# Seven transposes of the last chunks moved from TensorE to transposing transfers on SyncE's queue, in a kernel of an RWKV-7 recurrence and a squared-ReLU feed-forward network

## The chip, the cores and the metric

The kernel runs on one core of a Trainium2 chip. The metric is the device time of the whole program in microseconds, taken over several executions. A profiled execution gives, beside its own time, a span from the first to the last instruction; the rest of that execution's time lies around the span.

## The reference

For 4 batches of 8 heads, 768 steps and a head dimension of 40, a state of 40 x 40 per head is carried from step to step; then all heads' outputs go through a feed-forward network with squared ReLU.

```python
for t in range(S):
    y[:, :, t] = np.einsum('bhd,bhde->bhe', rt, state)
    Sa = np.einsum('bhde,bhe->bhd', state, at)
    state_decay = state * wt[:, :, None, :] - np.einsum('bhd,bhe->bhde', Sa, bt)
    state = state_decay + np.einsum('bhd,bhe->bhde', vt, kt)
...
h = x @ w_in              # x: 3072 tokens x 320, w_in: 320 x 2048
r = np.maximum(h, 0.0)
return (r * r @ w_out).astype(np.float32)
```

Inputs and output are float32; the kernel multiplies in bfloat16.

## The kernel before

The 768 steps are cut into 12 chunks (`c` = 0 to 11) of 64 steps (`L`), all 32 heads side by side. Each chunk goes through five functions that record named operations: `load` (`ldw`, `ldk`, `ldb`, `ldv`, `lda`, `ldr`: DMAs on SyncE's queue), `prep` (decays and turned copies), `rec` (the recurrence inside the chunk and the new state), `read` (the chunk's outputs) and `ffn`. An operation's name holds its kind, the chunk and a part: `TV 11` is the transpose of chunk 11's v and u.

What is to be turned, and who reads it:

- `TK c` (in `prep`): `KB`, k over b, scaled by the decay, is transposed by TensorE into PSUM, and `tK c` copies it to `KBT`. `EN c g0` and `EN c g1` read it.
- `TV c` (in `read`): `VU`, v over u, is transposed, and `tV c` copies it to `VUT`. `CX c g0` and `CX c g1` read it. u comes from `u1 c`, which follows `NU c`.
- `TS c` (in `rec`): the state after the chunk, `STb`, is transposed, and `tS c` copies it to `Sb`. `RS c+1` of the next chunk reads it.

From chunk 4 on each of these transposes is 32 TensorE instructions of 64 rows (line 394); chunks 0 to 3 (`WHOLE`) use 16 of 128 rows (line 397). All other matmuls are recorded at line 390. `F c u0` to `u3` and `FL c u0` to `u3` are the first product of the feed-forward network (8 and 4 matmuls), `f` and `q` the ReLU and the square, `O c u0` to `u3` the second product (8 matmuls each), `o c` its copy into `osb`, `st c` the store (two DMAs on SyncE's queue). For chunk 11 `O` is split in three (`OA`, `OB`, `OC`). `cf c` and `ci c` are products with a triangle of ones that sum the logarithms of the decay, `S`, `SC`, `AS`, `EV`, `NU`, `Y` small products of the recurrence, `XT` the transpose of the outputs for the network.

The weights are loaded at the start through buffers that are in use later (`lwi`, `lwl`, `lwo`) and cast (`cwi`, `cwl`, `cwo`).

There is no scheduler at run time: `ORDER` is a text that names every operation once with its engine (and, for TensorE, one of four PSUM slots), and `Plan.issue` records them in that order. Each engine, SyncE's queue among them, works through its own entries in order and waits for what each one reads. An engine may run ahead of another only as far as data and buffers allow. Two copies of most buffers are used in turn (`c % 2`).

TensorE's instructions have shapes of four kinds (64 or 128 rows by 64 or 128 columns, the `mode` of an operation).

Of the kernel before, what the change touches and what calls it, by code (L numbers as in the profile page):

```python
# [91 lines left out]
DVE mEN 0 g0; SP ldb 2; ACT castA 1; SP lda 2; PE2 EV 0; DVE bK 0; PE0 TA 1; ACT u0 0; SP ldv 1;
DVE tA 1 g1; ACT eg 1; PE NU 0; PE3 TK 1; POOL castR 0; ACT u1 0 g0; DVE tK 1 g0; ACT ln 2; PE1 TR
0; ACT u1 0 g1; POOL hi 2; DVE tA 1 g0; SP lwi 0 k1 x2; ACT tRw 0; POOL lo 2; DVE tK 1 g1; SP ldk
2; PE2 EN 1 g0; PE0 TV 0; ACT castB 2; DVE mEN 1 g0; POOL castA 2; SP ldw 3; PE3 S 0 g0; ACT tV 0;
PE S 0 g1; PE1 EN 1 g1; POOL castV 1 g1; DVE s 0 q0; PE2 BK 1; DVE s 0 q1; ACT castV 1 g0; PE0 ci
2; SP lwi 0 k0 x2; DVE mEN 1 g1; PE3 CX 0 g1; SP lwi 0 k1 x1; ACT exw 2; SP ldr 1; ACT castK 2;
DVE mCX 0 g1; PE0 cf 2; PE1 TK 2; ACT eg 2; SP lwi 0 k0 x3; PE3 AS 1; ACT ef 2; PE EV 1; SP lwi 0
k1 x0; DVE tK 2 g1; SP lwi 0 k0 x0; ACT bK 1; PE0 TS 0; DVE u0 1; SP lwi 0 k1 x3; SP lwi 0 k0 x1;
DVE tK 2 g0; ACT ln 3; PE NU 1; SP ldv 2; ACT tS 0; PE2 CX 0 g0; POOL hi 3; DVE mCX 0 g0; PE1 TA  # L100
2; POOL lo 3; SP lwl 0; ACT u1 1 g0; PE0 SC 1; DVE tA 2 g1; ACT u1 1 g1; PE S 1 g0; PE2 Y 0; DVE
tA 2 g0; POOL castR 1; SP ldk 3; PE S 1 g1; DVE y 0; PE3 TR 1; PE1 EN 2 g1; DVE yd 0; ACT tRw 1;
DVE s 1 q0; POOL cwi 0 k1h0; PE2 EN 2 g0; DVE mEN 2 g1; PE3 TV 1; POOL cwi 0 k0h0; DVE mEN 2 g0;
PE1 BK 2; ACT tV 1; DVE s 1 q1; POOL castV 2 g1; PE2 XT 0; SP lwo 0 x0; POOL castV 2 g0; DVE xt 0;
PE0 ci 3 h0; PE3 ci 3 h1; DVE bK 2; PE2 AS 2; ACT ei 3 h1; PE EV 2; DVE cwi 0 k1h1; POOL cwl 0;
ACT ei 3 h0; PE1 F 0 u0; SP lwo 0 x1; ACT u0 2; ACT ex 3 h0 g0; PE FL 0 u0; SP ldr 2; ACT ex 3 h0
g1; PE NU 2; DVE f 0 u0; ACT ex 3 h1 g0; PE0 CX 1 g1; ACT ex 3 h1 g1; ACT cwi 0 k0h1; SP lda 3;
PE3 FL 0 u1; DVE u1 2 g0; PE F 0 u1; DVE mCX 1 g1; ACT u1 2 g1; PE1 SC 2; SP ldb 3; PE S 2 g0; ACT
f 0 u1; PE2 cf 3; DVE cwo 0 x0; PE0 CX 1 g0; ACT ef 3; PE S 2 g1; DVE mCX 1 g0; POOL cwo 0 x1; PE3
TV 2; PE2 TS 1; DVE s 2 q0; ACT tV 2; SP lwo 0 x2; DVE s 2 q1; PE0 F 0 u2; DVE tS 1; SP lwo 0 x3;  # L110
PE FL 0 u2; ACT castR 2; SP ldv 3; PE1 RS 1; PE Y 1; ACT castA 3; PE2 FL 0 u3; ACT f 0 u2; PE F 0
u3; DVE mulKB 3 h0; POOL mulKB 3 h1; PE3 TA 3; DVE y 1; ACT f 0 u3; PE0 TR 2; DVE yd 1; DVE tA 3
g0; PE1 XT 1; ACT tRw 2; SP ldr 3; PE2 TK 3; DVE xt 1; ACT cwo 0 x2; DVE tA 3 g1; POOL cwo 0 x3;
PE1 FL 1 u1; DVE tK 3; SP ldw 4; PE F 1 u1; POOL q 0 u1; PE3 CX 2 g1; ACT f 1 u1; PE0 CX 2 g0; DVE
mCX 2 g1; PE2 F 1 u2; ACT castV 3 g0; POOL castV 3 g1; SP lwo 0 x4; PE FL 1 u2; DVE mCX 2 g0; PE3
EN 3 g0; ACT f 1 u2; PE1 F 1 u0; POOL castR 3; SP lwo 0 x5; DVE mEN 3 g0; POOL q 0 u0; PE0 EN 3
g1; SP ldk 4; PE FL 1 u0; PE2 RS 2; DVE mEN 3 g1; PE Y 2; PE3 AS 3; ACT ln 4; ACT f 1 u0; PE0 FL 1
u3; DVE hi 4; PE EV 3; DVE yd 2; DVE lo 4; PE F 1 u3; ACT u0 3; POOL cwo 0 x4; DVE y 2; SP lda 4;
PE NU 3; ACT f 1 u3; PE2 ci 4 h0; POOL cwo 0 x5; DVE u1 3 g0; PE1 TS 2; ACT ex 4 h0 g1; SP ldb 4;
POOL q 0 u2; ACT ei 4 h0; DVE u1 3 g1; PE0 O 0 u0; ACT ex 4 h0 g0; ACT tS 2; PE2 ci 4 h1; POOL q 0  # L120
u3; PE3 TV 3; SP lwo 0 x6; ACT ex 4 h1 g0; ACT ei 4 h1; PE1 SC 3; DVE tV 3; ACT ex 4 h1 g1; SP lwo
0 x7; PE S 3 g0; PE S 3 g1; POOL castA 4; SP ldw 5; PE2 TR 3; DVE s 3 q1; PE O 0 u1; ACT tRw 3;
DVE s 3 q0; POOL mulKB 4 h0; PE3 XT 2; PE2 CX 3 g0; ACT xt 2; PE1 cf 4; DVE mCX 3 g0; PE O 0 u2;
ACT ef 4; SP ldv 4; DVE mulKB 4 h1; ACT cwo 0 x6; PE2 TA 4; PE1 CX 3 g1; POOL cwo 0 x7; DVE tA 4
g1; PE3 TK 4; DVE tA 4 g0; POOL q 1 u1; ACT tK 4; PE O 0 u3; DVE mCX 3 g1; PE2 F 2 u0; SP ldw 6;
DVE o 0; ACT q 1 u2; PE3 F 2 u2; DVE q 1 u0; ACT ln 5; PE0 EN 4 g0; PE FL 2 u2; DVE mEN 4 g0; PE1
FL 2 u3; POOL hi 5; ACT f 2 u2; PE FL 2 u0; SP ldr 4; PE F 2 u3; POOL lo 5; ACT f 2 u0; PE3 RS 3;
DVE f 2 u3; SP ldb 5; PE Y 3; POOL castV 4 g0; PE2 FL 2 u1; PE0 cf 5; DVE yd 3; POOL castV 4 g1;
DVE y 3; PE1 EN 4 g1; ACT ef 5; PE F 2 u1; POOL q 2 u0; DVE mEN 4 g1; PE3 XT 3; SP lda 5; ACT f 2
u1; PE0 TS 3; DVE xt 3; ACT ln 6; PE3 ci 5 h1; SP ldk 5; DVE tS 3; PE2 ci 5 h0; ACT ei 5 h1; PE1  # L130
AS 4; POOL hi 6; PE EV 4; ACT ex 5 h1 g1; POOL castR 4; ACT ei 5 h0; PE0 O 1 u0; DVE u0 4; ACT ex
5 h1 g0; POOL q 1 u3; SP lda 6; ACT ex 5 h0 g1; ACT ex 5 h0 g0; PE NU 4; PE O 1 u1; ACT u1 4 g0;
SP ldw 7; POOL lo 6; ACT u1 4 g1; PE2 SC 4; PE S 4 g0; PE S 4 g1; POOL castA 5; DVE mulKB 5 h1;
PE1 TR 4; PE3 ci 6 h1; ACT tR 4 g1; POOL mulKB 5 h0; SP ldr 5; PE O 1 u2; DVE s 4 q0; ACT ei 6 h1;
PE O 1 u3; ACT ex 6 h1 g0; DVE s 4 q1; SP ldv 5; ACT tR 4 g0; POOL q 2 u1; ACT ex 6 h1 g1; PE2 TS
4; ACT o 1; PE3 cf 6; DVE tS 4; PE1 TA 5; ACT ef 6; PE0 TV 4; SP ldr 6; DVE tA 5 g1; POOL castA 6;
PE2 TK 5; DVE tA 5 g0; ACT tV 4; PE3 FL 3 u1; POOL castR 5; PE F 3 u1; DVE tK 5; SP ldb 6; PE1 F 3
u0; DVE f 3 u1; ACT ln 7; PE FL 3 u0; PE0 TR 5; POOL castV 5 g0; ACT f 3 u0; PE2 EN 5 g0; SP lda
7; PE3 FL 3 u3; DVE mEN 5 g0; POOL q 2 u2; PE F 3 u3; ACT tR 5 g1; ACT tR 5 g0; PE1 CX 4 g0; PE2
CX 4 g1; ACT f 3 u3; DVE mCX 4 g0; SP ldk 6; PE0 O 2 u0; POOL q 3 u1; ACT q 2 u3; DVE mCX 4 g1;  # L140
PE3 EN 5 g1; PE1 ci 6 h0; PE O 2 u1; ACT ex 6 h0 g0; SP st 0; DVE mEN 5 g1; ACT castV 5 g1; ACT hi
7; PE2 RS 4; PE Y 4; SP ldv 6; ACT ei 6 h0; POOL lo 7; PE3 AS 5; DVE yd 4; ACT ex 6 h0 g1; PE EV
5; DVE y 4; PE O 2 u2; ACT u0 5; DVE mulKB 6 h1; POOL mulKB 6 h0; ACT q 3 u0; PE2 TA 6; SP ldw 8;
PE NU 5; DVE tA 6 g1; PE O 2 u3; DVE tA 6 g0; ACT u1 5 g0; ACT u1 5 g1; PE2 ci 7 h1; DVE o 2; PE1
XT 4; PE3 TV 5; ACT ex 7 h1 g0; POOL castV 6 g0; ACT ex 7 h1 g1; DVE xt 4; PE0 TK 6; SP ldk 7; ACT
ei 7 h1; DVE tV 5; POOL castA 7; PE1 SC 5; ACT tK 6; PE S 5 g0; POOL q 3 u3; PE S 5 g1; PE2 F 4
u2; DVE s 5 q0; DVE s 5 q1; PE FL 4 u2; ACT castR 6; PE3 CX 5 g0; SP lda 8; PE0 F 3 u2; DVE mCX 5
g0; ACT f 4 u2; PE1 EN 6 g0; SP ldb 7; PE FL 3 u2; DVE mEN 6 g0; PE3 EN 6 g1; ACT f 3 u2; PE2 FL 4
u3; PE F 4 u3; DVE mEN 6 g1; ACT ln 8; PE0 CX 5 g1; PE1 FL 4 u1; ACT f 4 u3; SP st 1; PE F 4 u1;
DVE mCX 5 g1; ACT castV 6 g1; PE2 RS 5; SP ldw 9; PE3 AS 6; ACT f 4 u1; DVE q 3 u2; PE Y 5; PE EV  # L150
6; DVE y 5; POOL mulKB 7 h1; PE1 ci 7 h0; ACT u0 6; DVE yd 5; PE0 cf 7; SP ldr 8; ACT ei 7 h0; PE
NU 6; ACT ex 7 h0 g0; PE2 O 3 u0; DVE u1 6 g0; ACT ex 7 h0 g1; ACT ef 7; SP ldv 7; DVE mulKB 7 h0;
PE O 3 u1; ACT u1 6 g1; DVE q 4 u1; PE0 TA 7; PE3 TR 6; PE1 TK 7; SP ldk 8; ACT tR 6 g0; PE O 3
u2; DVE tK 7; ACT hi 8; ACT tR 6 g1; POOL lo 8; PE O 3 u3; DVE tA 7 g0; DVE tA 7 g1; PE3 XT 5; ACT
o 3; PE1 TV 6; POOL castV 7 g1; DVE xt 5; PE0 ci 8 h0; ACT castR 8; DVE tV 6; PE2 SC 6; PE S 6 g0;
ACT ex 8 h0 g1; PE S 6 g1; ACT ei 8 h0; PE3 F 5 u0; DVE s 6 q0; SP ldr 10; ACT ex 8 h0 g0; DVE s 6
q1; PE FL 5 u0; PE0 CX 6 g1; ACT f 5 u0; PE1 TS 5; DVE mCX 6 g1; SP ldb 8; PE2 FL 5 u1; PE F 5 u1;
# [929 lines left out]
```

## Time and profile before

| what | us |
|---|---|
| median of 3 runs | 245.29 (245.1 to 246.02) |
| the profiled execution | 245.21 |
| its span | 242.8 |
| TensorE busy in it | 223.2 |
| VectorE, ScalarE, GpSimd busy | 182.8, 178.8, 119.9 |

Engines in the profile: PE is TensorE's matmul, PEld its weight loads, DVE is VectorE, ACT ScalarE, POOL GpSimd, SP SyncE; a name with q (SPq, ACTq) is that engine's queue, where it issues or waits. A row of a timeline has the start in us, the time from the first start to the last end, engine, line, operation, written and read tiles, and how many instructions it merges. Since matmuls overlap, the step from one row's start to the next row's start is what a row costs TensorE, and its duration is a little longer.

### The profile page before, as it was taken

The numbers are of one execution on the slowest core, as the hardware profiler recorded it, in microseconds if no ns is written. First come the engines' busy times: TensorE is split into PE (matmuls) and PEld (weight loads), VectorE is DVE, ScalarE is ACT, GpSimd is POOL, SyncE is SP. The second block draws the span as 40 slices with busy tenths as digits, with TensorE's granted clock in tenths as the row PEclk, the third lists the DMA queues.
The fourth block names the chain that finished last, engine by engine and source line by source line (L and its number), as shares of the span: only waits on it lengthen the run. The fifth ranks groups of instructions, "written<-read, shape, count | busy, mean of one in ns | idle before, by whom it ended". The sixth has DMA issues, their size and how long they took to land.

```text
span 242.8 us, 12250 instructions
## 1 busy us (share of the span) xinstructions
PE 223.2 (92%) x5584; PEld 175.7 (72%) x5584; DVE 182.8 (75%) x227; ACT 178.8 (74%) x231; POOL 119.9 (49%) x110
## 2 busy tenths in 40 slices
PE   0587698899999999999999999999999999999994
...
DMA  6989899989978979997864957788457020000403
GB/s 144 232 165 211 191 248 188 227 186 209 196 182 135 196 160 185 184 178 143 173 113 95 223 117 121 186 143 153 106 109 136 6 57 5 3 5 0 100 11 107
DMA packets 102248, 33.54 MB, mean 138 GB/s; under 512 B 89014, under 2 KB 101814, under 8 KB 101942
## 3 DMA queue, kind: packets, MB, share of 16 engines
q1 hardware_dynamic: 101014, 32.45, 64.9%
...
HBM read 28.84 MB, written 3.93 MB: 135 GB/s over the span
## 4 chain that ended last, share of the span: by engine, by line
PE 77%; SPq 9%; DMA 5%; ACT 2%; issue 2%; POOL 2%; DVE 1%; POOLq 0%; ACTq 0%
PE pb L390 66%; PE pb L394 7%; PE pb L397 4%; SPq L1003 2%; SPq L1011 2%; DMA raw_w<-in_w_dram 2%; DMA CX<-in_moe_w_in_dram 2%; SPq L453 2%; SPq L413 1%; SPq L421 1%; DMA raw_r<-in_r_dram 1%; DVE EN L689 1%; SPq L436 1%; POOL lo L384 1%; DVE CX L689 1%
## 5 line engine op out<-in xcount | busy, mean ns | idle before, releaser
L936 POOL TENSOR_TENSOR G<-G 128x1024 bf16<-128x1024 bf16 x24 | 45.7, 1909 | 32.2 <-ACT G L928 29.9
L390 PE MATMUL pb<-WOUT,G 128*128 128x320 bf16 (+1 forms) x400 | 57.0, 294 | 0.0
L928 ACT ACTIVATE G<-pb 128x1024 bf16<-128x1024 f32 x39 | 39.5, 1022 | 15.4 <-PE pb L390 15.3
L390 PE MATMUL pb<-XT,WIN 128*128 128x256 bf16 x384 | 48.4, 273 | 0.0
L390 PEld LDWEIGHTS <-G 128*128 128x128 bf16 x400 | 36.3, 98 | 13.7 <-issue 0.8
L390 PEld LDWEIGHTS <-WIN 128*128 128x128 bf16 x384 | 34.7, 98 | 8.1 <-issue 3.6
L689 DVE TENSOR_TENSOR CX<-pb,MSKI 128x1024 bf16<-128x1024 f32 x24 | 29.0, 1219 | 5.5 <-PE pb L390 5.4
L689 DVE TENSOR_TENSOR EN<-pb,MSK 128x1024 bf16<-128x1024 f32 x24 | 28.9, 1218 | 3.2 <-PE pb L390 3.0
L384 POOL TENSOR_TENSOR KB<-raw_kb,iG 128x640 bf16<-128x640 f32 x13 | 21.3, 1641 | 9.0 <-DMA raw_kb<-in_b_dram 8.3
L781 DVE TENSOR_TENSOR STb<-pb,GT 64x640 bf16<-64x640 f32 x22 | 18.0, 820 | 2.7 <-PE pb L390 2.4
L658 DVE TENSOR_TENSOR AR<-pb,GT 128x512 bf16<-128x512 bf16 x24 | 15.7, 686 | 5.2 <-PE pb L394 2.4
L384 POOL TENSOR_TENSOR lo<-lnW,hi 128x640 bf16<-128x640 f32 x9 | 13.2, 1466 | 11.4 <-ACT hi L376 11.0
L574 ACT ACTIVATE Gin<-pb 64x320 f32<-64x320 f32 x36 | 15.5, 429 | 4.3 <-PE pb L390 3.8
L390 PE MATMUL pb<-XT,WLAST 64*128 64x256 bf16 x192 | 17.1, 271 | 0.6 <-POOL WLAST L380 0.4
L390 PEld LDWEIGHTS <-EN 64*64 64x64 bf16 x768 | 14.8, 112 | 2.7 <-issue 1.6
L376 ACT ACTIVATE AR<-pb 128x512 bf16<-128x512 bf16 (+1 forms) x17 | 11.4, 694 | 6.7 <-PE pb L394 2.9
L859 DVE TENSOR_TENSOR Yb<-pb,Gin 128x640 bf16<-128x640 f32 (+1 forms) x24 | 12.4, 550 | 4.1 <-PE pb L390 4.1
L938 ACT ACTIVATE G<-G 128x1024 bf16<-128x1024 bf16 x15 | 15.5, 1052 | 0.0
L390 PE MATMUL pb<-UTI,hi 64*128 64x64 bf16 x192 | 8.2, 198 | 8.0 <-DVE hi L371 7.5
L930 DVE TENSOR_SCALAR G<-pb 128x1024 bf16<-128x1024 f32 x9 | 11.0, 1220 | 5.3 <-PE pb L390 5.3
L568 ACT ACTIVATE iG<-pb 128x640 f32<-128x640 f32 x18 | 12.5, 700 | 2.7 <-PE pb L390 2.5
L380 POOL CAST hi<-lnW 128x640 bf16<-128x640 f32 x7 | 5.0, 719 | 18.2 <-ACT lnW L532 9.5
...
## 6 DMA issues: line engine op xcount, KB each, us to landing
raw_kb<-in_k_dram SPq DMA_DIRECT2D x24, 160.0 KB, 4.4
raw_kb<-in_b_dram SPq DMA_DIRECT2D x24, 160.0 KB, 4.5
raw_a<-in_a_dram SPq DMA_DIRECT2D x24, 160.0 KB, 3.9
raw_v<-in_v_dram SPq DMA_DIRECT2D x24, 160.0 KB, 4.7
raw_w<-in_w_dram SPq DMA_DIRECT2D x23, 160.0 KB, 4.9
raw_r<-in_r_dram SPq DMA_DIRECT2D x22, 160.0 KB, 4.2
out_dram<-osb SPq DMA_DIRECT2D x22, 160.0 KB, 3.3
osb<-in_moe_w_out_dram SPq DMA_DIRECT2D x8, 320.0 KB, 6.1
```

What stands on the lines that cost most here:

```text
L384: return [("POOL", 40 + 2.35 * n, lambda: nc.gpsimd.tensor_tensor(out=o_(), in0=a_(), in1=b_(), op=op)), ("DVE", c_dve(n), lambda: nc.vect ...
L390: return lambda: nc.tensor.matmul(out=o_(), lhsT=l_(), rhs=r_(), start=start, stop=stop, skip_group_check=True)
L394: return lambda: nc.tensor.transpose(out=o_(), in_=i_(), identity=IDb[rows(g), :])
L568: ew(f"ei {c} h{jh}", [("ACT", c_act(2 * n), lambda hb=hb, jh=jh: nc.scalar.activation(out=iG[0][:].rearrange("p (g j) e -> p g (j e)", g= ...
L574: nc.scalar.activation(out=Gin[c % NGI][rows(g), NP * jh:NP * jh + NP, :].rearrange("p j e -> p (j e)"), in_=slot(hb, FP32)[rows(g), g, 0: ...
L658: ew(f"tA {c} g{g}", [("DVE", c_dve(512), lambda g=g: nc.vector.tensor_tensor(out=steps(AR[q2][:, 0, g]), in0=turned(ha, g), in1=steps(GT[ ...
L689: evac(f"m{nm} {c} g{g}", lambda s, n: [("DVE", c_dve(n), lambda: nc.vector.tensor_tensor(out=dst[q2][:, g, s].rearrange("p q i t -> p (q ...
L781: ew(f"s {c} q{q}", [("DVE", c_dve(2 * n), lambda q=q: nc.vector.tensor_tensor(out=STb[q2][rows(q), :, q, 0:D], in0=slot(hs, FP32)[rows(q) ...
L859: return [("DVE", c_dve(2 * (f1 - f0)), lambda: nc.vector.tensor_tensor(out=Yb[q2][:, :, to:to + f1 - f0], in0=slot(hy, FP32)[:, :, f0:f1] ...
L928: ("ACT", c_act(1024), lambda gb=gb, hf=hf: nc.scalar.activation(out=gb, in_=slot(hf, FP32)[:], func=ACTF.Relu)),
L936: ("POOL", 1900, lambda gv=gv: nc.gpsimd.tensor_tensor(out=gv, in0=gv, in1=gv, op=ALU.mult)),
L938: ("ACT", c_act(1024), lambda gv=gv: nc.scalar.activation(out=gv, in_=gv, func=ACTF.Square))],
```

## The change

`dma_start_transpose` on SyncE's queue takes the place of the seven operations `TK 11`, `TV 9`, `TV 10`, `TV 11`, `TS 8`, `TS 9`, `TS 10` and of the copies out of PSUM behind them. Each moves 128 partitions x 2048 bfloat16 elements (512 KB) from SBUF to SBUF as 16 blocks of 128 x 128. `Sb` gets rows of 64 instead of 40 elements, and its readers and writers take the first 40.

```diff
+    DTK, DTV, DTS = range(11, 12), range(9, 12), range(8, 11)
...
-    Sb = buf("Sb", [128, NJ, 2, D], BF16, 2)
+    Sb = buf("Sb", [128, NJ, 2, 64], BF16, 2)
...
+    def turn(name, out_, in_, reads, writes):
+        plan.add(name, [("SP", 750)], ("ew", {"SP": lambda: nc.sync.dma_start_transpose(
+            out=out_(), in_=in_())}), reads=reads, writes=writes)
...
-        if c not in RUNS:
+        if c in DTK:
+            turn(f"dK {c}", lambda: KBT[q2][:].rearrange("p j x t -> p j (x t)"),
+                 lambda: KB[c % NK][:].rearrange("p h e -> p (h e)"), KBK, [("KBT", q2)])
+        if c not in RUNS and c not in DTK:
             hb = ("A", "TK", c)
...
+            if c in DTS:
+                turn(f"dS {c}", lambda: Sb[q2][:].rearrange("p i q e -> p i (q e)"),
+                     lambda: STb[q2][:].rearrange("p i q e -> p i (q e)"),
+                     [("STb", q2, 0), ("STb", q2, 1)], [("Sb", q2)])
+                return
             ht = ("A", "TS", c)
...
-        hb = ("A", "TV", c)
...
+        if c in DTV:
+            turn(f"dV {c}", lambda: VUT[q2][:].rearrange("p j x t -> p j (x t)"),
+                 lambda: vu[:].rearrange("p h e -> p (h e)"), VU0 + VU1, [("VUT", q2)])
+        else:
+            hb = ("A", "TV", c)
...
-                                 lambda p=p, g=g: Sb[(c - 1) % 2][:, NP * g + p].rearrange(
-                                     "p q e -> p (q e)"), p % 4 == 0, False))
+                                 lambda p=p, g=g: Sb[(c - 1) % 2][:, NP * g + p, :, 0:D],
+                                 p % 4 == 0, False))
```

`ORDER` is another text from its first line on (1025 entries instead of 1032). Of SyncE's queue the end reads, before and after:

```
before: ... lda 11; st 6; st 5; ldv 11; ldr 11; ldk 11; ldb 11; st 7; st 9; st 8; st 10; st0 11 g1; st0 11 g0
after:  ... lda 11; ldb 11; dS 8; st 5; ldk 11; ldv 11; dV 9; dS 9; dK 11; st0 0; st 6; dV 10; st 8; dV 11; dS 10; st 7; st 9; st 10; st0 11 g1; st0 11 g0
```

TensorE's entries between `NU 11` and the readers of the last two transposes, after the change: `NU 11; F 9 u3; RS 10; Y 10; F 9 u0; FL 9 u1; FL 9 u0; XT 10; F 9 u1; F 10 u2; FL 10 u1; FL 10 u2; FL 10 u3; F 10 u3; F 10 u1; F 10 u0; CX 11 g0; CX 11 g1; O 9 u0; O 9 u1; RS 11`. Between `u1 9` and `CX 9 g0` they are, behind `F 7 u1`: `F 8 u0; EN 10 g0; FL 8 u0; SC 9; S 9 g0; S 9 g1; cf 11; FL 8 u1; ci 11 h0; F 8 u1; AS 10; EV 10; O 7 u0; O 7 u1; O 7 u2; NU 10; CX 9 g0`; from there on `CX 9 g1; O 7 u3; O 8 u0; TA 11; SC 10; RS 9; S 10 g0; Y 9; S 10 g1; O 8 u1; O 8 u2; XT 9; EN 11 g0; TR 10; O 8 u3; TR 11; EN 11 g1; F 9 u2; FL 9 u2; AS 11; EV 11; CX 10 g1; CX 10 g0; FL 9 u3; NU 11`.

At the start, TensorE's first product with the weights, `F 0 u0`, stands before the change behind `ci 3 h0; ci 3 h1; AS 2; EV 2`, with `cf 3` and both `CX 1` later; after the change `cf 3` and `CX 1 g0` stand ahead of `F 0 u0`. In both texts the same 18 loads of chunks 0 to 3, `ldw 0` to `ldw 3`, three each of k, b, a and v, two of r, and the eight `lwi` stand ahead of `lwl 0` in SyncE's queue.

More of the change, by code (lines that the diff above doesn't have):

```diff
@@ L92 @@
[L92 to L157, printed above, removed]
@@ new lines @@
+mEN 1 g1; PE3 BK 1; POOL castV 1 g1; DVE s 0 q0; PE2 EN 1 g0; ACT bK 1; PE0 CX 0 g1; DVE mCX 0 g1;
+SP lwi 0 k1 x3; ACT castV 1 g0; PE3 cf 2; SP lwi 0 k0 x3; POOL castA 2; DVE s 0 q1; PE0 ci 2; ACT
+eg 2; SP ldr 1; DVE mEN 1 g0; PE1 TK 2; ACT exw 2; SP lwi 0 k0 x1; ACT ef 2; DVE tK 2 g0; PE0 AS
+1; SP lwi 0 k0 x0; PE EV 1; SP lwi 0 k1 x2; PE2 CX 0 g0; DVE tK 2 g1; ACT u0 1; PE3 TA 2; SP lwi 0
+k1 x1; ACT ln 3; PE NU 1; SP lwi 0 k0 x2; DVE mCX 0 g0; PE1 TS 0; ACT u1 1 g0; SP ldv 2; ACT u1 1
+g1; DVE tA 2 g0; SP lwl 0; DVE hi 3; PE2 TV 1; DVE tA 2 g1; POOL lo 3; DVE tS 0; PE0 SC 1; SP lwo
@@ new lines @@
+PE0 F 2 u2; ACT o 0; DVE q 1 u1; SP ldw 6; ACT ln 5; DVE f 2 u0; PE1 EN 4 g0; PE3 FL 2 u3; PE FL 2
+u2; POOL hi 5; PE F 2 u3; ACT f 2 u2; DVE mEN 4 g0; POOL lo 5; PE2 RS 3; ACT f 2 u3; PE Y 3; SP
+ldr 4; PE1 FL 2 u1; POOL q 1 u0; DVE y 3; PE0 EN 4 g1; PE3 cf 5; DVE yd 3; SP ldb 5; PE F 2 u1;
+DVE mEN 4 g1; ACT ef 5; PE2 XT 3; POOL castV 4 g0; ACT f 2 u1; PE3 TS 3; SP lda 5; DVE xt 3; POOL
+q 2 u3; ACT castV 4 g1; PE2 ci 5 h1; DVE tS 3; PE1 ci 5 h0; ACT ex 5 h1 g1; PE0 AS 4; ACT ex 5 h0
+g0; PE EV 4; ACT ei 5 h1; POOL q 2 u2; PE3 O 1 u0; SP ldk 5; DVE u0 4; ACT ex 5 h1 g0; ACT ln 6;
```

207 lines of the change are left out of this document (131 added, 76 removed).

## The prediction

> **What bounds the kernel now.** I read the page's busy times and slices first, then the windows, then the chain of waits, and last the timeline of TensorE and the DMA rows.
>
> ```profile
> span 242.8 us, 12250 instructions
> ...
> PE 223.2 (92%) x5584; PEld 175.7 (72%) x5584; DVE 182.8 (75%) x227; ACT 178.8 (74%) x231; POOL 119.9 (49%) x110
> ...
> PE   0587698899999999999999999999999999999994
> ...
> DMA  6989899989978979997864957788457020000403
> GB/s 144 232 165 211 191 248 188 227 186 209 196 182 135 196 160 185 184 178 143 173 113 95 223 117 121 186 143 153 106 109 136 6 57 5 3 5 0 100 11 107
> ```
>
> TensorE (PE) has the most work and from the tenth slice on, at some 55 us, hardly a pause. The DMA engines are crowded at the start and nearly free in the last quarter, where the change puts its transfers. The windows put numbers to both:
>
> ```profile
> core 0: us, PE busy (x) PEld busy (x) DVE busy (x) ACT busy (x) POOL busy (x), PEclk, DMA share, GB/s
> 0.00:45.00 45.00, 29.80 (x787) 24.26 (x787) 35.71 (x54) 28.64 (x34) 20.58 (x34) 0.96 0.92 197
> 75.00:120.00 45.00, 45.00 (x1196) 34.80 (x1196) 36.94 (x43) 39.13 (x52) 31.29 (x25) 1.00 0.85 166
> 120.00:160.00 40.00, 39.75 (x1072) 30.70 (x1065) 31.54 (x39) 31.73 (x43) 22.46 (x16) 1.00 0.71 146
> 200.00:210.00 10.00, 10.00 (x327) 8.05 (x321) 7.78 (x10) 5.93 (x6) 0.03 (x1) 1.00 0.02 5
> 210.00:220.00 10.00, 10.00 (x296) 8.33 (x295) 7.63 (x10) 6.76 (x7) 3.76 (x2) 1.00 0.02 3
> ```
>
> PE is busy 45.00 of 45.00 us from 75 to 120, and 10.00 of 10.00 in the stages where the transposes go, at a granted clock of 1.00. Only the first 45 us have slack (29.80 busy), and there the DMA share is 0.92. The chain of waits says the same:
>
> ```profile
> 31.37 0.42 SPq L1011
> ...
> 40.62 4.59 DMA CX<-in_moe_w_in_dram
> ...
> 45.36 1.05 POOL WLAST L380
> ...
> 46.45 4.47 PE pb L390 x148
> ...
> 205.21 0.47 PE pb L394 x32
> ...
> 221.59 17.79 PE pb L390 x164
> 239.38 0.02 issue
> 239.40 0.30 ACT osb L376
> ```
>
> Up to 46.45 it runs through loads (the last of the first weights lands at 45.21); from there to 239.38 it is matmuls nearly throughout. One of its pieces, 32 transposes at line 394 in 0.47 us, is of the kind that goes. So work taken from PE shortens the end one for one, as long as what replaces it lands before PE comes to its reader.
>
> **The change part by part.** *Removed from PE.* The steps from one row to the next:
>
> ```profile
> 191.56 0.19 PE L390 MATMUL pb<-UTI,hi 64*128 64x64 bf16 x2
> ...
> 192.13 2.35 PE L390 MATMUL pb<-WOUT,G 128*128 128x320 bf16 x16
> ...
> 204.81 0.41 PE L390 MATMUL pb<-AR,VUT 64*128 64x64 bf16 x16
> 205.05 0.63 PE L394 MATMUL pb<-IDb,STb 64*128 64x64 bf16 x32
> 205.51 0.40 PE L390 MATMUL pb<-AR,KBT 64*128 64x64 bf16 x16
> ...
> 212.02 1.92 PE L390 MATMUL pb<-XT,WIN 128*128 128x256 bf16 x16
> 213.87 0.35 PE L394 MATMUL pb<-IDb,Yb 64*128 64x64 bf16 x12
> 214.06 0.63 PE L394 MATMUL pb<-IDb,VU 64*128 64x64 bf16 x32
> 214.53 0.63 PE L394 MATMUL pb<-IDb,STb 64*128 64x64 bf16 x32
> 215.09 1.05 PE L390 MATMUL pb<-XT,WIN 128*128 128x256 bf16 x8
> ```
>
> `TV 11` takes 214.53 - 214.06 = 0.47 us, a `TS` 205.51 - 205.05 = 0.46. Seven of them: 7 x 0.47 = 3.3 us. Their copies out of PSUM go too (seven operations of VectorE and ScalarE); I count nothing for that, since neither engine ends the time while PE is full.
>
> *The new order's changes of shape.* A `TS` that is followed by a product of another shape costs 215.09 - 214.53 = 0.56 instead of 0.47, so a change costs about 0.1 us. Counting TensorE's entries, neighbours of different shape go from 198 to 201: 3 x 0.1 = 0.3 us more. Bounds: 0 and 0.6.
>
> *The new order's start.* `cf 3` and `CX 1 g0` now stand ahead of `F 0 u0`, in the stretch in which PE waits for weights. By the rows above a `cf` takes 192.13 - 191.56 = 0.57 us at most, with the change of shape behind it, and a `CX` 205.05 - 204.81 = 0.24. About 0.7 us of work is thus done in time that was idle. Ahead of `lwl 0`, the last load PE waits for, SyncE's queue holds the same 18 loads and eight weight pieces in another sequence, so I leave its landing where it is. Bounds for the start as a whole: 1.5 us either way, the size of a load's place in that queue. I take -0.7.
>
> *`Sb` in rows of 64.* `RS` then reads two runs of 40 instead of one of 80. `AS` already reads `STb` that way, and both take the same:
>
> ```profile
> 208.92 0.48 PE L390 MATMUL pb<-STb,AR 128*64 128x80 bf16 x16
> ...
> 218.93 0.48 PE L390 MATMUL pb<-Sb,AR 128*64 128x80 bf16 x16
> 219.24 0.66 PE L390 MATMUL pb<-KB,CX 128*64 128x40 bf16 x32
> 219.83 1.26 PE L390 MATMUL pb<-WOUT,G 128*128 128x320 bf16 x8
> ```
>
> So nothing, with PE's own time as the measure.
>
> *The seven transfers.* No row shows a transposing transfer. The nearest:
>
> ```profile
> q1 hardware_dynamic: 101014, 32.45, 64.9%
> ...
> out_dram<-osb SPq DMA_DIRECT2D x22, 160.0 KB, 3.3
> osb<-in_moe_w_out_dram SPq DMA_DIRECT2D x8, 320.0 KB, 6.1
> ```
>
> A store of 160 KB lands 3.3 us after its issue. At the best rate of any slice, 248 GB/s, 163,840 bytes take 0.66 us, which leaves 2.6 us that do not depend on size. 524,288 bytes at that rate take 2.1 us, so a transfer lands after 2.1 + 2.6 = 4.7 us: my value, because in this stage the other traffic is 2% of the DMA engines. The lower bound is the store's 3.3. For the upper one I go by packets: 101,014 of them took 64.9% of 16 x 242.8 us, 25 ns each. In pieces of 256 bytes (a row of one block) 2048 packets take 2048 x 25 / 16 = 3.2 us, landing 5.8; in pieces of 32 bytes 16,384 take 25.6 us, landing 28. I choose by bytes and not by the smallest pieces, because the row nearest in size, 320 KB in 6.1 us in the crowded stage, is already near the former.
>
> *What covers them.* A late transfer stalls its reader on PE, and everything on PE stands behind that reader. `dV 11` starts when `u1 11` is written. Until `CX 11 g0` PE then has `RS 10` and `Y 10` (219.83 - 218.93 = 0.90), six `F` (two take 213.87 - 212.02 = 1.85, so 5.55), five `FL` (next fence, four in 0.98: 1.23) and `XT 10` (214.06 - 213.87 = 0.19): 7.9 us. The two `u1` copies outlast the `F 9 u3` that runs beside them by some 0.5 us: 7.4 us of cover against 4.7.
>
> ```profile
> 222.63 3.42 PE L390 MATMUL pb<-WOUT,G 128*128 128x320 bf16 x24
> 225.89 1.91 PE L390 MATMUL pb<-XT,WIN 128*128 128x256 bf16 x16
> 227.73 1.05 PE L390 MATMUL pb<-XT,WLAST 64*128 64x256 bf16 x16
> 228.71 1.92 PE L390 MATMUL pb<-XT,WIN 128*128 128x256 bf16 x16
> ```
>
> `dS 10` is issued behind `dV 11`; its reader `RS 11` stands behind two `CX 11` and two steps of `O 9` (three take 225.89 - 222.63 = 3.26, so 2.17), at 7.4 + 0.5 + 2.2 = 10.1 us, against 2 x 2.1 + 2.6 = 6.8. `dV 9` has, by the same rows, three steps of `O`, two `F` and small products in front of `CX 9 g0`, about 8.5 us. `dK 11`, third in the queue, has four more steps of `O` (4.35), `RS` and `Y` (0.90) and small products up to `EN 11 g0`, about 15.5 us after `dV 9` starts; from there to `CX 10 g1`, the reader of `dV 10`, it is a step of `O`, an `F`, an `FL` and small products, about 4.8. Every cover holds at my price. Behind the waiting `dV 9` stand `dS 9`, `dK 11` and the stores `st 6`, `st 8`; behind `dS 10` stands `st 7`. `o 8` and `o 9` wait for these stores, several steps of PE later, so I count nothing; without that cover each store costs its 3.3 us once.
>
> [...]
>
> *The sum.* -3.3 + 0.3 - 0.7 = -3.7 us on a span of 242.8: 239.1. The profiled execution's 245.21 has 2.41 us around its span: 241.5. It stands 0.08 below the median of 245.29, so I forecast 241.6.
>
> **The rivals.** *A, the forecast:* 241.6, between 240.6 and 243.4 by the bounds of the order's terms.
>
> *B, no gain:* the new sequence of loads at the start, or a store or load held up behind a waiting transfer on the queue, gives back the 3.7 us; 245.3. For it: the first 45 us go by transfers (share 0.92), and each us that `lwl 0` lands later is a us at the end. Against it: the same loads stand ahead of `lwl 0`.
>
> *C, slower:* the transfers themselves become the bound, in the last four chunks. With X the time that one holds the queue, the point is 2X + 2.6 = 10.1, X = 3.75 us, 1.8 times my value; beyond it `RS 11` stalls, then the others in turn. At X = 6: `dV 9` lands after 8.6, 0.1 late; `dK 11`, third, after 20.6 against 15.5, 5.0 more; `dV 10`, 6.0 behind it against 4.8, 1.2 more; `dV 11` 8.6 against 7.4, 1.2; `dS 10` 14.6 against 10.1, 3.3 beyond that. Together 10.8: 241.6 + 10.8 = 252.4. In pieces of 32 bytes (X = 25.6) six transfers in a row would cost over 100 us. For it: no row prices a transposing transfer, and seven of 512 KB are long transfers. Against it: the empty queue at that stage.
>
> **How the numbers follow.** A 0.63, B 0.12, C 0.25. About 0.5% (1.2 us) is what a measurement of this kernel can tell from no change, so faster means below 244.1: A and a little of B, 0.65; slower above 246.5: C, 0.25; the rest 0.10. The likeliest case's own range is 240.6 to 243.4. To leave out no more than 2 in 10, the range takes in B and the cheaper half of C, up to 251; C's dearer half lies outside.
>
> **What would show it.** PE's instructions fall from 5584 to 5360 and its busy time by about 3 us. The chain stays on PE to the end if the covers hold; if C is right it passes through a DMA of `VUT`, `Sb` or `KBT`, and PE shows idle time ended by it before line 390. The time from issue to landing of the seven transfers should be 4 to 6 us; over 7.4 the forecast is wrong. The start is judged by when the chain goes over to PE for good, 46.45 before: later than 48 speaks for B.

## The result and the profile after

| what | us |
|---|---|
| changed kernel, median of 20 executions | 244.44 (243.31 to 247.7) |
| kernel before, 20 executions beside them | 245.99 (243.96 to 248.0) |
| ratio, 95% interval | 0.9941 (0.9917 to 0.9965) |
| forecast | 241.6, a ratio of 241.6 / 245.29 = 0.985 |

The change makes the kernel faster, by 0.6% or 1.5 us; 3.7 us were forecast. On the scale of the 245.29 of before it takes 243.8, just outside the forecast's own range (240.6 to 243.4) and inside the whole one.

The first profiled execution of the changed kernel was a disturbed one (247.7 us), so the rows "after" below come from a second profile of the same kernel, which ran 242.34 us with a span of 240.6. First the page's busy times, its DMA slices and its busiest queue (packets, MB, share):

```profile
span 240.6 us, 11789 instructions
...
PE 221.0 (92%) x5360; PEld 174.1 (72%) x5360; DVE 186.3 (77%) x232; ACT 171.9 (71%) x224; POOL 110.4 (46%) x105
...
DMA  7998999997889969885487788885994994292204
...
q1 hardware_dynamic: 115574, 36.13, 75.3%
```

PE has the forecast's 5360 instructions, and 2.2 us less busy time. The queue carries 115,574 - 101,014 = 14,560 packets and 3.68 MB more, some 250 bytes a packet. The DMA slices of the last quarter, nearly empty before, are filled in part. The windows of the same execution, in the stages shown of before and two more:

```profile
core 0: us, PE busy (x) PEld busy (x) DVE busy (x) ACT busy (x) POOL busy (x), PEclk, DMA share, GB/s
0.00:45.00 45.00, 29.95 (x798) 24.54 (x800) 37.32 (x58) 31.34 (x38) 18.56 (x32) 0.98 0.96 203
75.00:120.00 45.00, 44.92 (x1176) 35.31 (x1176) 35.87 (x42) 37.14 (x49) 31.94 (x27) 1.00 0.76 149
120.00:160.00 40.00, 39.98 (x1086) 31.54 (x1087) 31.94 (x37) 31.63 (x44) 21.64 (x17) 1.00 0.83 165
180.00:190.00 10.00, 9.37 (x252) 7.15 (x250) 9.55 (x10) 8.75 (x13) 9.78 (x9) 1.00 0.59 107
190.00:200.00 10.00, 9.98 (x239) 7.70 (x239) 6.30 (x9) 5.43 (x7) 4.44 (x3) 1.00 1.08 174
200.00:210.00 10.00, 9.99 (x282) 7.61 (x279) 8.02 (x8) 5.98 (x10) 0.00 (x0) 1.00 0.25 55
210.00:220.00 10.00, 10.00 (x140) 7.66 (x136) 6.47 (x8) 6.71 (x7) 3.79 (x2) 1.00 0.82 139
```

Where the transfers run (190 to 220) PE stays full although the DMA share is up to 1.08. Of the last four stages only 180 to 190 has a hole, 9.37 of 10.00, and there VectorE (9.55) and GpSimd (9.78) are both full. The chain of waits of this execution passes through that hole:

```profile
185.54 0.64 POOL tR L380
...
186.22 1.90 POOL G L953
188.12 1.86 POOL VU L380
...
190.02 7.48 PE pb L390 x135
...
222.60 14.52 PE pb L390 x136
237.15 0.30 ACT osb L376
```

From 190.02 to 237.15 it is on PE. No transfer into `VUT`, `Sb` or `KBT` is on it, but a copy on GpSimd (line 380, `castV 10 g1`) is: a wait that the prediction does not have.

**The transfers.** SyncE's queue between the first and the last of them (start, time that the queue was held), one row of what the trace says of `VUT`, and PE's rows at the covers of the last two:

```profile
171.86 3.99 SPq L471 DMA_TRANSPOSE Sb<-STb  x1
...
185.24 1.79 SPq L471 DMA_TRANSPOSE VUT<-VU  x1
188.71 2.96 SPq L471 DMA_TRANSPOSE Sb<-STb  x1
191.77 3.15 SPq L471 DMA_TRANSPOSE KBT<-KB  x1
...
196.93 2.30 SPq L471 DMA_TRANSPOSE VUT<-VU  x1
...
209.65 2.02 SPq L471 DMA_TRANSPOSE VUT<-VU  x1
211.77 2.44 SPq L471 DMA_TRANSPOSE Sb<-STb  x1
```

```profile
VUT<-VU SPq DMA_TRANSPOSE x3, 6.1
```

```profile
217.09 0.64 PE L390 MATMUL pb<-AR,VUT 64*128 64x64 bf16 x32
...
219.94 0.48 PE L390 MATMUL pb<-Sb,AR 128*64 128x80 bf16 x16
```

One holds the queue for 1.8 to 4.0 us, median 2.4 (forecast 2.1), and the page has one landing time, 6.1 us after the issue, for `VUT` (forecast 4.7; three other profiles gave 5.3 to 6.2). The cover of `dV 11` is 217.09 - 209.65 = 7.4 us, as forecast, so by a landing of 6.1 us 1.3 us of it were left. The pair `dV 11` and `dS 10` held the queue from 209.65 to 214.21, 4.6 us, where the forecast had 4.2. The dearest single ones took 3.15 and 3.99 us.

### The profile page after: what moved, and what is told of

It is laid out like the page before. It is cut to its first block, busy times and chain, and to the rows that moved or that the text cites. A ratio compares the mean times of both kernels' runs of the same rounds, so it can differ in the third digit from the quotient of the medians.

```text
span 246.0 us, 11789 instructions
## 1 busy us (share of the span) xinstructions
PE 221.8 (90%) x5360; PEld 174.7 (71%) x5360; DVE 186.6 (76%) x232; ACT 171.8 (70%) x224; POOL 110.9 (45%) x105
## 3 DMA queue, kind: packets, MB, share of 16 engines
q1 hardware_dynamic: 115574, 36.13, 74.2%
## 4 chain that ended last, share of the span: by engine, by line
PE 76%; DVE 8%; issue 7%; ACT 5%; POOL 2%; POOLq 0%; ACTq 0%; DVEq 0%
PE pb L390 65%; PE pb L394 6%; PE pb L397 5%; ACT Gin L578 1%; DVE KBT L516 1%; POOL VU L380 1%; DVE CX L696 1%; ACT VUT L376 1%; DVE EN L696 1%; DVE IDQ L314 1%; ACT iG L572 1%; DVE STb L788 1%; ACT lnW L536 1%; POOL tR L380 1%; ACT KB L376 1%
## 5 line engine op out<-in xcount | busy, mean ns | idle before, releaser
L953 POOL TENSOR_TENSOR G<-G 128x1024 bf16<-128x1024 bf16 x21 | 40.1, 1912 | 38.8 <-ACT G L945 38.4
L384 POOL TENSOR_TENSOR lo<-lnW,hi 128x640 bf16<-128x640 f32 x9 | 12.6, 1400 | 21.0 <-DVE hi L371 8.6
L384 POOL TENSOR_TENSOR KB<-raw_kb,iG 128x640 bf16<-128x640 f32 x8 | 12.9, 1619 | 19.3 <-ACT iG L572 9.9
L380 POOL CAST VU<-raw_v 64x640 bf16<-64x640 f32 x16 | 14.5, 907 | 6.8 <-DMA raw_v<-in_v_dram 6.3
L376 ACT ACTIVATE VU<-pb 64x640 bf16<-64x640 f32 x18 | 12.6, 697 | 6.5 <-PE pb L390 5.9
L390 PE MATMUL pb<-XT,WLAST 64*128 64x256 bf16 x192 | 16.4, 271 | 0.0
L955 ACT ACTIVATE G<-G 128x1024 bf16<-128x1024 bf16 x14 | 14.5, 1051 | 0.3 <-DVE G L947 0.2
```

What stands on the lines that cost most here:

```text
L376: alts.append(("ACT", c_act(n), lambda: nc.scalar.activation(out=o_(), in_=i_(), func=ACTF.Copy, scale=1.0 if scale is None else scale)))
L380: lambda: nc.gpsimd.tensor_copy(out=o_(), in_=i_())))
L384: return [("POOL", 40 + 2.35 * n, lambda: nc.gpsimd.tensor_tensor(out=o_(), in0=a_(), in1=b_(), op=op)), ("DVE", c_dve(n), lambda: nc.vect ...
L390: return lambda: nc.tensor.matmul(out=o_(), lhsT=l_(), rhs=r_(), start=start, stop=stop, skip_group_check=True)
L953: ("POOL", 1900, lambda gv=gv: nc.gpsimd.tensor_tensor(out=gv, in0=gv, in1=gv, op=ALU.mult)),
```

## The experiments

Each number is a median, and each ratio is to the kernel before run beside it (244.98 us for the first four, 244.81 for the next three).

One measure is used throughout. The matmuls of a profile, counted off in the sequence of `ORDER`, tell when each operation began. The old order and the new one have the same 290 operations ahead of `F 8 u2`, and all seven transposes stand behind it. They also have the same first 57 operations, `F 0 u0` and both `CX 1` among them. So PE's time up to these points, and from `F 8 u2` to the last matmul, can be compared between orders (us; profiles a and b are of further executions, reported below):

```
                        57 operations   start of   last      from F 8 u2
                        done at         F 8 u2     matmul    to the last
before                          52.66     179.43   239.13          59.70
before, profile a               53.13     179.38   239.09          59.71
before, profile b               53.28     181.39   241.09          59.70
old order, less                 54.77     182.30   241.50          59.20
changed, first profile          54.72     185.01   242.25          57.24
changed                         52.33     179.63   236.88          57.25
changed, profile b              53.60     181.08   238.33          57.25
no transfers                    52.16     179.32   236.57          57.25
order alone                     52.24     179.50   241.59          62.09
copy moved                      53.77     181.61   238.03          56.42
copy moved, profile b           53.62     181.26   237.68          56.42
transfers twice                 53.15     181.05   246.91          65.86
```

The last column repeats to 0.01 us from one profile of a kernel to the next. The first 180 us do not: they differ by 2 us among the profiles of before and by more among those of the changed kernel.

**The changed kernel again, as the measure for the others.**

> The changed kernel once more, for a second profile: the first one (span 246.0 us) has TensorE's first product with the weights at 47.12 us where it was 45.00 before, and TensorE idle for 2.9 us inside one transpose at 40 us with no releaser in the trace. Theory S (the new order's start gives the gain back): the first product with WIN begins 1.5 to 2 us later than before here too. Theory T (the transfers give it back): the start is within 0.7 us of before's, and TensorE's losses lie between 175 and 215 us, where the transfers are. Both: 0.4 to 0.8% faster than before.

243.43 us, ratio 0.9948 (0.991 to 0.9986). The gain is there again, and again small against 3.7 us. `F 0 u0` starts at 46.22, 1.2 us later than before, between what the two theories said.

**Are the transfers covered?** They are left out, with no transpose in their place: their readers take an older chunk's turned copy.

```diff
     def turn(name, out_, in_, reads, writes):
-        plan.add(name, [("SP", 750)], ("ew", {"SP": lambda: nc.sync.dma_start_transpose(
-            out=out_(), in_=in_())}), reads=reads, writes=writes)
+        return
```

The seven entries of SyncE leave the order, and all others stay.

> The changed order with the seven transposing transfers left out and nothing in their place (the last chunks read stale turned copies, so the output is wrong). Theory T (transfers crowd the DMA engines, 0.93 of them from 180 to 200 us against 0.15 to 0.60 before, and so delay casts and loads that TensorE waits for): about 3.7 us below before, 242.3 where before has 246.0. Theory S (the start of the new order gives it back): no different from the changed kernel, about 1.5 us below before.

242.62 us, ratio 0.9914 (0.9877 to 0.9951), an interval that overlaps that of the changed kernel; the spans are 240.2 and 240.6. From `F 8 u2` to the last matmul it is 57.25 us with the transfers and without. So the seven transfers cost PE nothing there, and what eats the gain is elsewhere; whether the 0.8 us between the two medians is more than noise is not settled. PE's stop for `castV 10 g1` stands in this profile too:

```profile
187.75 4.55 POOL L380 CAST VU<-raw_v 64x640 bf16<-64x640 f32 x3
...
189.71 0.65 PE L390 MATMUL pb<-VU,EN 64*64 64x40 bf16 x31 [0.65 <-POOL VU L380]
```

**The new order alone.** The seven transposes and their copies come back, close to their readers.

```diff
-    DTK, DTV, DTS = range(11, 12), range(9, 12), range(8, 11)
+    DTK, DTV, DTS = (), (), ()
```

> The changed order with all seven transposes back on TensorE and their copies on VectorE or ScalarE, and no transfer. Theory S: the new order is slower than before by what it gives back, 1.8 us above before. Theory T: the order by itself is worth its start, 0 to 0.7 us below before. TensorE's work is 3.3 us more than in the changed kernel in either case.

248.0 us, ratio 1.0115 (1.0062 to 1.0168): 3.0 us above before, slower than either theory said, and 4.6 above the changed kernel. The loss is not at the start: 57 operations are done at 52.24. From `F 8 u2` on PE takes 62.09 us, 4.8 more than in the changed kernel. The seven transposes are 3.3 of it; among the rest are waits for the copies out of PSUM, which stand close in front of their readers here: 0.31 us for `Sb` and 0.17 for `KBT`. In this order taking the transposes out is thus worth its 3.3 us and more.

**The old order without the fourteen operations.** Nothing in their place.

```diff
-        if c not in RUNS:
+        if c not in RUNS and c != 11:
...
+            if c in range(8, 11):
+                return
...
-        pe(f"TV {c}", *tmode(c), ms, reads=VU0 + VU1, writes=[hb], alloc=[hb])
+        if c not in range(9, 12):
+            pe(f"TV {c}", *tmode(c), ms, reads=VU0 + VU1, writes=[hb], alloc=[hb])
```

> The order of before with the seven transposes and their copies left out, nothing in their place (stale turned copies, wrong output). If TensorE's work counts one for one, as forecast: 3.3 us below before. Rival (the order of before fits every engine so closely that TensorE, freed, waits for ScalarE and VectorE at NU 9, SC 9, NU 10, XT 9 and F 10): 0.5 to 1.0 us below before, with TensorE idle for some 2.5 us more after 175 us.

244.19 us, ratio 0.998 (0.994 to 1.002): no gain that can be told, as the rival said. PE has 5360 instructions here too. From `F 8 u2` on it takes 59.20 us against 59.70; the seven transposes took 3.57 there, with the changes of shape behind three of them, so 3.07 of it went into waits. (This profile is of an execution of 247.02 us; what it has over the median lies ahead of `F 8 u2`.) Its timeline of PE has pauses that the kernel before does not have, among them:

```profile
190.69 0.46 PE L389 MATMUL pb<-STb,IDQ 128*64 128x320 bf16 x4 [0.55 <-ACT Gin L573]
...
199.05 0.41 PE L393 MATMUL pb<-IDb,tR 64*128 64x64 bf16 x16 [0.20 <-DVE AR L657]
...
208.38 1.03 PE L389 MATMUL pb<-XT,WIN 128*128 128x256 bf16 x8 [0.22 <-ACT osb L375]
```

The longest, 0.65 us in front of `F 10`, is at 217.47 for VectorE's copy into `XT`. The removed transposes had stood in front of waits: PE at 10.00 of 10.00 hid copies that ended just in time. In this kernel the work taken from the full engine became time only where the order put other work in its place.

**One copy moved, the rest as changed.** `castV 10 g1` goes ahead of the square `q 7 u0` on GpSimd.

```diff
-u0; POOL q 7 u0; PE S 9 g0; PE S 9 g1; PE1 cf 11; DVE s 9 q1; ACT q 8 u3; PE0 FL 8 u1; PE3 ci 11
-h0; DVE s 9 q0; PE F 8 u1; POOL castV 10 g1; ACT ex 11 h0 g0; ACT ei 11 h0; DVE mulKB 11 h1; POOL
+u0; POOL castV 10 g1; POOL q 7 u0; PE S 9 g0; PE S 9 g1; PE1 cf 11; DVE s 9 q1; ACT q 8 u3; PE0 FL
+8 u1; PE3 ci 11 h0; DVE s 9 q0; PE F 8 u1; ACT ex 11 h0 g0; ACT ei 11 h0; DVE mulKB 11 h1; POOL
```

> The changed kernel with one entry moved: GpSimd's cast of chunk 10's v, castV 10 g1, ahead of the square q 7 u0 instead of behind it. In four profiles of the new order that cast takes 1.91 us instead of 0.72 beside VectorE's products from SBUF, and EV 10 stands still for 0.85 us until it ends. If that wait is a loss at the end: TensorE's pause inside EV 10 goes, the cast takes 0.7 us, and the time is 0.8 to 0.9 us below the changed kernel (about 1.0% below before). Rival: the next operation waits in its place, and the time is that of the changed kernel.

242.2 us, ratio 0.9862 (0.9802 to 0.9921), the lowest median of all versions. Below is what stood at the hole in the changed kernel, then the same place here; GpSimd's rows, VectorE's and PE's:

```profile
186.22 1.90 POOL L953 TENSOR_TENSOR G<-G 128x1024 bf16<-128x1024 bf16 x1
188.06 3.77 POOL L380 CAST VU<-raw_v 64x640 bf16<-64x640 f32 x2
188.57 0.81 DVE L386 TENSOR_TENSOR KB<-raw_kb,iG 128x640 bf16<-128x640 f32 x1
189.30 1.22 DVE L951 TENSOR_TENSOR G<-G 128x1024 bf16<-128x1024 bf16 x1
190.02 0.65 PE L390 MATMUL pb<-VU,EN 64*64 64x40 bf16 x31 [0.65 <-POOL VU L380]
```

```profile
188.18 0.71 POOL L380 CAST VU<-raw_v 64x640 bf16<-64x640 f32 x1
188.86 1.89 POOL L953 TENSOR_TENSOR G<-G 128x1024 bf16<-128x1024 bf16 x1
...
191.15 0.68 PE L390 MATMUL pb<-VU,EN 64*64 64x40 bf16 x32
191.76 0.45 PE L390 MATMUL pb<-WOUT,G 128*128 128x320 bf16 x2
```

In the changed kernel the copy starts at 188.06 and the row of two takes 3.77 us; moved, it takes 0.71, and `EV 10` (the 32 instructions that read `VU` and `EN`) runs through: 0.61 us instead of 1.44. Four more profiled executions on one chip took 245.09 and 247.19 us for the kernel before, 243.88 for the changed one and 243.12 for this one:

> The kernel of before, for a second profile. Theory F (TensorE's first 50 us go by the arrival of its instructions, so that the order of before and the new one reach the same amount of work at the same time, whatever stands ahead of the first product with WIN): TensorE pauses at matmul 734 here too, 0.7 to 2 us, and its losses up to the first product with WIN are 11 to 13 us in both kernels. If the new order's start is worth the 0.7 us of the forecast: its losses there are 0.7 us below those of before.

> The same once more: a third profile of before, for the spread of the first 90 us. Same expectations.

> The changed kernel, a third profile. Theory F: a pause of 1.5 to 3.4 us at matmul 734 (in XT 0), losses up to the first product with WIN as in before within the spread of the profiles, and between 90 us and the end 0.5 to 1 us more lost than before, nearly all of it in EV 10.

> The version with the cast of chunk 10's v ahead of the square, a second profile: from 150 to 200 us TensorE loses 1.4 to 1.6 us as in before, where the changed kernel loses 2.3; the pause at matmul 734 stays.

Two executions of before differ by 2.1 us there, so these times alone tell nothing of 0.8. The part from `F 8 u2` on does: 57.25 us in both of these profiles of the changed kernel, 56.42 in both of this one. The wait in `EV 10` costs 0.83 us, and nothing waits in its place. At the start all four are alike, as theory F said: the 57 operations are done at 53.13 to 53.62 us. Over all executions the two intervals of the medians still overlap (0.991 to 0.9921).

**What stops PE at the start.** Between 40 and 44 us PE stands still with "issue" as the reason, that is, for nothing that the profile shows; in the changed kernel inside `XT 0`:

```profile
40.75 0.27 PE L397 MATMUL pb<-IDQ,Yb 128*128 128x128 bf16 x2
42.75 0.38 PE L397 MATMUL pb<-IDQ,Yb 128*128 128x128 bf16 x4 [1.73 <-issue]
...
44.03 0.74 PE L390 MATMUL pb<-STb,AR 128*64 128x80 bf16 x16
44.70 1.04 PE L390 MATMUL pb<-VU,EN 64*64 64x40 bf16 x32
45.68 0.61 PE L390 MATMUL pb<-AR,VUT 64*128 64x64 bf16 x16
46.22 1.12 PE L390 MATMUL pb<-XT,WIN 128*128 128x256 bf16 x8
```

The page lists a queue of instructions (q8) with 42 packets in 0.69 MB, 16,384 bytes each. With two instructions a matmul (its weight load and itself), 5360 of each in 42 packets are 255 a packet, and the 5584 of each in the 43 packets of before 260: by this estimate a piece is 256 instructions, or 128 matmuls. The stop is at a fixed number in PE's stream, 734 = 94 + 5 x 128, in both orders. The trace gives the packet of that piece and the matmul that follows (a gap is from the start of one matmul to the next):

```
                       packet us   it took   PE goes on   after a gap of
before                   40.75       1.33       43.60          0.75
before, profile a        40.01       1.43       43.04          2.00
before, profile b        40.27       1.45       43.09          1.52
changed                  39.84       1.45       42.75          1.94
changed, profile b       40.07       1.48       43.06          3.00
no transfers             38.97       1.56       42.37          2.64
copy moved               40.26       1.47       43.05          3.32
copy moved, profile b    39.95       1.45       43.05          2.97
```

PE goes on 1.3 to 1.8 us after the packet's end, between 42.4 and 43.6 us in these eight profiles (at 41.99 in the order alone), and what differs is how long it has stood still by then. To tell the stream's place from `XT 0` itself, 64 small matmuls on a tile of ones go in front of everything:

```diff
+        t = ps.tile([128, 2, 512], FP32, name="pb3", tag="pb3", bufs=1)
+        for _ in range(64):
+            nc.tensor.matmul(out=t[:, 0, 0:64], lhsT=ones[:], rhs=ones[:, 0:64], start=True,
+                             stop=True, skip_group_check=True)
```

> The changed kernel with 64 small matmuls on constants in front of everything, in the time in which TensorE has nothing to do yet. Theory F (TensorE runs out of instructions: they come in pieces of 16,384 bytes, 256 instructions, and around 40 us the next piece lands 7 us after the one before was begun, while TensorE gets through one in 5): the pause of 1.5 to 3 us at matmul 734 leaves XT 0, which is matmul 798 now, and stands 64 matmuls earlier in the order, again at number 734 of the stream, again 1.5 to 3 us; the total does not change by more than 0.5 us. Rival (XT 0 itself waits for something the trace does not show): the pause stays at XT 0.

Ratio 1.0006 (0.996 to 1.0053). The pause leaves `XT 0`, which runs its instructions in a row; so it was not that operation. At 734, where the expectation had 1.5 to 3 us, there is only a step of 0.36 (at 37.68 us); somewhat later PE now stands still for two copies into `VU` (0.69 and 1.36 us at 43 to 44.6). But new pauses stand at the numbers 2140, 2523 and 2779 (gaps of 0.93, 1.00 and 0.86 us at 99.67, 114.20 and 124.05), each within five of 94 + 128 j, in stages that were full before. All thirteen profiles kept say the same: 30 steps of over 0.35 us stand inside an operation with no releaser, and all 30 lie within four matmuls of 94 + 128 j, where 7% of all matmuls are. That the stops lie at these boundaries is shown. That the start's total would stay was a miss: by the ratios the version is 1.4 us slower than the changed kernel, where at most 0.5 was expected. That the delay lies in the packets is read from their times; no run changed those.

**What does it cost when the covers are too short?** Each transfer is issued twice, first into a spare buffer.

```diff
+        def both_of():
+            nc.sync.dma_start_transpose(out=to[:], in_=in_())
+            nc.sync.dma_start_transpose(out=out_(), in_=in_())
-        plan.add(name, [("SP", 750)], ...
+        plan.add(name, [("SP", 1500)], ("ew", {"SP": both_of}), reads=reads, writes=writes)
```

> The changed kernel with each of the seven transfers issued twice, first into a spare buffer, then where it is needed. One holds SyncE's queue for 2.0 us and lands 6.1 us after its issue in the trace. If the covers are as the forecast counted them (7.4 us for dV 11, 10.1 for dV 11 and dS 10 together, 15.5 for dV 9, dS 9 and dK 11): with 2.4 us a transfer TensorE waits before EN 11 (about 1.4 us), CX 11 (about 1.0) and RS 11 (about 2.1), and the time is about 4.5 us above the changed kernel. Rival (the covers are much longer than counted): no more than 0.5 us above it.

251.74 us, ratio 1.0266 (1.0208 to 1.0324). PE's timeline, with the idle time before each row and what ended it:

```profile
196.95 0.64 PE L390 MATMUL pb<-AR,VUT 64*128 64x64 bf16 x32 [0.89 <-DMA VUT<-VU]
...
206.93 0.41 PE L390 MATMUL pb<-AR,KBT 64*128 64x64 bf16 x16 [2.48 <-DMA KBT<-KB]
...
214.11 0.64 PE L390 MATMUL pb<-AR,VUT 64*128 64x64 bf16 x32 [2.45 <-DMA VUT<-VU]
...
229.97 0.48 PE L390 MATMUL pb<-Sb,AR 128*64 128x80 bf16 x16 [1.14 <-DMA Sb<-STb]
```

This is rival C made real: four readers wait, 7.0 us in all, and the time is 8.3 above the changed kernel where 4.5 was expected. Two transfers held the queue for 4.6 to 6.3 us, median 5.7, not the 4.8 assumed. The prediction's case X = 6 had 10.8 us, with `dK 11` dearest, as it is here beside `dV 10`; `CX 11 g0`, which it had 1.2 us late, does not wait at all, since the waits ahead of it left the queue time. From `F 8 u2` on PE takes 65.86 us, 8.6 more than in the changed kernel. The other 1.6 us come with a granted clock of 0.50 from 215.4 to 218.8, behind the wait that ended at 214.11.

## Why the prediction was wrong in its size

**-3.3 for the seven transposes: right, and 0.8 of it taken back.** With the copy moved, the part from `F 8 u2` on is 59.70 - 56.42 = 3.28 us shorter than before: the term as forecast. In the changed kernel it is 59.70 - 57.25 = 2.45.

**+0.3 for changes of shape: not told.** The new order has as many changes behind `F 8 u2` as the old one (43); its three more stand ahead of it, where profiles of one kernel differ by 2 us.

**The covers: right, with a smaller reserve.** The choice "by bytes" (4.7 us) was the wrong one of the two: the packets have about the 256 bytes of the upper bound (5.8), and the landing was 6.1. No reader waited, and the covers themselves were well counted: `CX 9 g0` started 9.4 us after `dV 9` was issued (forecast 8.5, and 0.8 of it is the wait in `EV 10`), `CX 10 g1` 4.7 us after `EN 11 g0` (4.8), `CX 11 g0` 7.4 after `dV 11` (7.4), `RS 11` 10.3 (10.1). That `Sb` in rows of 64 costs nothing fits too: `RS 11` takes 0.48 us as before.

**-0.7 for the start: this step failed.** The prediction put "about 0.7 us of work" into "time that was idle" and judged the start by loads. It is idle, but by the packets' times PE comes out of it when its next piece of instructions is there, at 42 to 43.6 us in both orders. `AS 2` then starts at 44.03, 43.98 before, with `cf 3` already done: that half of the step held. But an earlier arrival at the boundary was a longer pause there, and near it PE was granted a clock of 0.50 in seven of the eight profiles of the table above. The 57 operations are done at 52.66 to 53.28 us in the three profiles of before and at 52.16 to 54.72 in the eight of the new order, with a median of 53.4: no gain of 0.7. The windows (the last three columns are the granted clock, the DMA share and GB/s) of before, of the changed kernel, and of another profile of the kernel before:

```profile
43.00:45.00 2.00, 1.54 (x56) 1.05 (x53) 1.66 (x3) 0.86 (x2) 0.73 (x2) 1.00 0.96 171
45.00:47.00 2.00, 1.59 (x31) 1.03 (x28) 0.04 (x1) 1.96 (x5) 1.04 (x1) 1.00 1.14 212
```

```profile
43.00:45.00 2.00, 2.00 (x63) 1.76 (x62) 1.52 (x3) 1.42 (x3) 0.00 (x0) 0.50 1.25 217
45.00:47.00 2.00, 2.00 (x51) 1.74 (x48) 1.54 (x3) 1.17 (x3) 0.00 (x0) 0.65 1.05 143
```

```profile
43.00:45.00 2.00, 1.90 (x43) 1.42 (x45) 0.00 (x0) 1.24 (x2) 1.29 (x2) 0.54 1.05 194
45.00:47.00 2.00, 2.00 (x27) 1.40 (x25) 0.00 (x0) 1.54 (x5) 1.04 (x1) 0.60 1.17 191
```

After the gap of 0.75 us the clock stayed at 1.00; after those of 1.94 and 2.00 it was 0.50. In the changed kernel `AS 2` and `EV 2` step 0.67 and 0.98 us instead of 0.40 and 0.62, and `CX 1 g0` 0.54 instead of the 0.34 it takes at full clock: 0.8 us, the size of what the step was to bring. `F 0 u0` starts 1.22 later with `cf 3` and `CX 1 g0` ahead of it. But the kernel before has such stretches too: the third pair is of it, and its first profile has one from 31.4 to 34.8. What may differ is how long they are: before had one of 3.4 us in each of its three profiles, the changed kernel one of 3.4 and, in profile b, one of 6.8. One of 3.4 us lowers the mean clock of an execution by 0.007 (0.50 x 3.4 of some 242 us). The length of the pause alone does not decide: profile b of before had its stretch with a gap of 1.52, and the order alone kept its clock after one of 1.53. PE was busy 1.42 of the 3.42 us ahead of the stretch of the changed kernel, and 2.11 of 3.42 at the same place in the order alone. What starts such a stretch is not shown.

**The medians.** The two profiled spans differ by 2.2 us, the medians of the times by 1.5. Part of that 1.5 is outside the span: the time around it is 2.2 us in 44 executions of before and 1.7 in 32 of the changed kernel (medians), where the prediction kept its 2.41. Those 0.5 us were luck, and why they went is open. The spans thus differ by about 1.0, while the part from `F 8 u2` on is 2.45 shorter in every profile. So, by this estimate, the first 180 us took some 1.4 us longer in the new order on average, where the prediction had -0.7 + 0.3. The mean granted clock is 0.9918 over those executions of before and 0.9874 over those of the changed kernel: at most 0.0044 x 241 = 1.1 us of work, by an estimate that takes all of PE's work to follow its clock. That more time at half rate is the cause is argued, not shown: no run held the pauses fixed.

**+0.8 that no step has: the wait in `EV 10`.** This step failed too: a term put at nothing. The new order does not only move PE's work. It gives `castV 10 g1`, ScalarE's before, to GpSimd behind a square, while two products `mulKB 11`, GpSimd's before, go to VectorE. PE comes to `EV 10` before the copy is done; `EV 10` takes 1.44 us instead of 0.61, with and without transfers, and 0.61 with the copy moved. The prediction followed the queue of SyncE and the order of PE, and counted nothing for the other engines, since "neither engine ends the time while PE is full". The runs in the old order and with the copy moved show the opposite: a full PE waited for ScalarE and VectorE there, and for GpSimd here, once the margin was used up.

**The sum again.** Forecast: -3.3 + 0.3 - 0.7 = -3.7. In the two profiles shown: -3.3 + 0.8 for `EV 10`, and +0.2 up to `F 8 u2`, -2.25 at the last matmul. Over the executions: -3.3 + 0.8 + about 1.4 up to `F 8 u2`, and -0.5 outside the span: about -1.5. Of the rivals, C's mechanism exists but not at this price. B named the right place, the start, with another cause: what the traces show there is no load but the stops at the pieces of instructions. Its sign, a chain that goes over to PE later than 48, came and went: at 53.02 in the profile shown, through a load that PE waited 0.2 us for, and at 43.06 in profile b.
